# Loading K first, grouping the value products, and accumulating the output projection in PSUM in a one-core decode kernel

## The chip, the cores and the metric

The kernel runs on one core of one Trainium2 chip. Times are device microseconds (us) of a whole execution; a profile's "span" (from its first to its last instruction) is about 1.9 us shorter. The 16 runs of the kernel before lie between 85.12 and 85.53 us. Now and then a run takes longer, and only fast runs are compared. PE is TensorE, PEld its weight loads, DVE VectorE, ACT ScalarE, SP SyncE, which issues the transfers here.

## The reference

One decode step: layer norm of x (512 values), attention of 32 heads over a window of 1024 cached keys and values each, plus a feed-forward network, plus the residual.

```python
xn = _layernorm(x)                                  # x: 1 x 1 x 512
q = (xn @ wq)                                       # wq: 512 x 4096, 32 heads of 128
k, v = k_cache[:, :, Sk-W:, :], v_cache[:, :, Sk-W:, :]     # W = 1024 of Sk = 4096
o = softmax(q k^T * 128**-0.5) v                    # per head
A = o.reshape(1, 1, 4096) @ wo                      # wo: 4096 x 512
B = relu(xn @ w1 + b1)**2 @ w2 + b2                 # w1: 512 x 1376, w2: 1376 x 512
return x + A + B
```

Everything is bf16. Every weight and cache byte is used once: 28.0 MB are read, 8 MiB each for K and V, 4 MiB each for wq and wo, 2.7 MiB for w1 and w2.

## The kernel before

All large loads go out on one queue (SP) in the order wq, w1, w2, K, wo, V. PE transposes K (DVE copies each pair of heads back to SBUF), forms the scores, the softmax follows for all heads at once, and then the heads are taken one by one.

```python
small = ctx.enter_context(tc.tile_pool(name="small", bufs=1))     # many small tiles
wff   = ctx.enter_context(tc.tile_pool(name="wff", bufs=1))       # w1, w2
wbig  = ctx.enter_context(tc.tile_pool(name="wbig", bufs=4))      # wq, later wo
kv    = ctx.enter_context(tc.tile_pool(name="kv", bufs=1))        # K, V
# ... loads: wq, w1, w2, K (8 chunks of 4 heads), wo (4), V (16 chunks of 2 heads) ...
for h in range(Hq):
    g = h // 8
    for j in range(NJ):                                   # 8 matmuls, one column out
        nc.tensor.matmul(oT_ps[:, h : h + 1], lhsT=V_all[:, h, j, :], rhs=E[:, h, j : j + 1], ...)
    nc.vector.tensor_tensor(out=oTs[:, h : h + 1], in0=oT_ps[:, h : h + 1], in1=rb_sb[:, h : h + 1], op=ALU.mult)
    for bl in range(ND):                                  # 4 matmuls, each to its own column
        nc.tensor.matmul(attn_ps[:, bl, h : h + 1], lhsT=wo_t[g][:, h - 8 * g, bl * P : (bl + 1) * P],
                         rhs=oTs[:, h : h + 1], start=True, stop=True)
attn_sum = small.tile([P, ND], F32, name="attn_sum")
nc.vector.tensor_reduce(out=attn_sum[:, :], in_=attn_ps[:, :, :], axis=AX.X, op=ALU.add)
fin_bf = small.tile([P, ND], BF16, name="fin_bf")
nc.vector.tensor_tensor(out=fin_bf[:, :], in0=attn_sum[:, :], in1=ffn_ps[:, :], op=ALU.add)
# ... transpose on PE, copy to frow, transfer out ...
```

Note for later how the pools lie: the small tiles come first in each SBUF partition, each on a slot rounded up to 32 bytes (attn_sum has 16 bytes and takes 32), and the large tiles that the transfers fill lie directly behind them. The compiled program of the kernel before gives these start addresses in a partition: w1 at 22816, w2 at 33824, the four wq/wo buffers from 45088, K at 77856, V at 143392. Each is 32 more than a multiple of 256.

Of the kernel before, what the change touches and what calls it, by code (L numbers as in the profile page):

```python
# [9 lines left out]
ALU = mybir.AluOpType  # L10
AX = mybir.AxisListType
BF16 = mybir.dt.bfloat16
F32 = mybir.dt.float32
# [3 lines left out]
def kernel(  # L17
# [14 lines left out]
    nc = tc.nc  # L32
    P = 128

    _, _, D = A_x.shape
    _, Hkv, Sk, Dh = A_k_cache.shape
    Hq = 32
# [4 lines left out]
    Sk0 = Sk - W  # L42
    NJ = W // P
    ND = D // P
    NF = (F + P - 1) // P
    F_full = (NF - 1) * P
    F_last = F - F_full
    NG = Hq // 8
    KCH = 4
    VCH = 2  # L50
# [3 lines left out]
    dq = nc.sync  # L54
# [3 lines left out]
    small = ctx.enter_context(tc.tile_pool(name="small", bufs=1))  # L58
    wff = ctx.enter_context(tc.tile_pool(name="wff", bufs=1))
    wbig = ctx.enter_context(tc.tile_pool(name="wbig", bufs=4))  # L60
    kv = ctx.enter_context(tc.tile_pool(name="kv", bufs=1))
    ktsbp = ctx.enter_context(tc.tile_pool(name="ktsbp", bufs=2))
    psA = ctx.enter_context(tc.tile_pool(name="psA", bufs=1, space=bass.MemoryType.PSUM))

    wq_t = []
    for i in range(ND):
        t = wbig.tile([P, HD], BF16, name=f"wq{i}", tag="w")
        dq.dma_start(out=t[:, :], in_=A_wq[i * P : (i + 1) * P, :])
        wq_t.append(t)
    w1_sb = wff.tile([P, ND, F], BF16, name="w1_sb")  # L70
    dq.dma_start(out=w1_sb[:, :, :], in_=B_w1.rearrange("(i p) f -> p i f", p=P))
    w2_sb = wff.tile([P, NF, D], BF16, name="w2_sb")
    dq.dma_start(
        out=w2_sb[:, 0 : NF - 1, :],
        in_=B_w2[0:F_full, :].rearrange("(c p) d -> p c d", p=P),
    )
    dq.dma_start(out=w2_sb[0:F_last, NF - 1, :], in_=B_w2[F_full:F, :])  # L77
    K_all = kv.tile([P, Hq, NJ, Dh], BF16, name="K_all")
    for g in range(Hq // KCH):
        dq.dma_start(  # L80
            out=K_all[:, KCH * g : KCH * (g + 1), :, :],
            in_=A_k_cache[0, KCH * g : KCH * (g + 1), Sk0:Sk, :].rearrange("h (p j) d -> p h (j d)", p=P),
        )
    wo_t = []
    for g in range(NG):
        t = wbig.tile([P, 8, D], BF16, name=f"wo{g}", tag="w")
        dq.dma_start(out=t[:, :, :], in_=A_wo[g * 8 * Dh : (g + 1) * 8 * Dh, :].rearrange("(h d) c -> d h c", d=Dh))  # L87
        wo_t.append(t)
    V_all = kv.tile([P, Hq, NJ, Dh], BF16, name="V_all")
    for g in range(Hq // VCH):  # L90
        dq.dma_start(
            out=V_all[:, VCH * g : VCH * (g + 1), :, :],
            in_=A_v_cache[0, VCH * g : VCH * (g + 1), Sk0:Sk, :].rearrange("h (p j) d -> p h (j d)", p=P),
        )

    x_row = small.tile([1, D], BF16, name="x_row")
# [1 line left out]
    x4 = small.tile([ND, P], BF16, name="x4")  # L98
    dq2.dma_start(out=x4[:, :], in_=A_x[0, 0, :].rearrange("(c p) -> c p", p=P))  # L99
    b2_4 = small.tile([ND, P], BF16, name="b2_4")  # L100
# [6 lines left out]
    ident_bf = consts.tile([P, P], BF16, name="ident_bf")  # L107
# [11 lines left out]
    c_hT = c_b1T + NF  # L119
    c_qT = c_hT + NF  # L120
    assert c_qT + Hq <= 512
    aux_ps = psA.tile([P, 512], F32, name="aux_ps")
    S_ps = aux_ps[:, c_S : c_S + Hq * NJ].rearrange("p (h j) -> p h j", j=NJ)
    ffn_ps = psA.tile([P, ND], F32, name="ffn_ps")

    stats = small.tile([1, nc.vector.BN_STATS_DIM], F32, name="stats")
    nc.vector.bn_stats(out=stats[:, :], in_=x_row[:, :])
# [16 lines left out]
    b1T_sb = small.tile([P, NF], F32, name="b1T_sb")  # L144
    nc.vector.tensor_copy(out=b1T_sb[:, :], in_=aux_ps[:, c_b1T : c_b1T + NF])  # L145
    xnT = small.tile([P, ND], BF16, name="xnT")
    nc.vector.tensor_scalar(  # L147
        out=xnT[:, :],
        in0=aux_ps[:, c_xT : c_xT + ND],
        scalar1=mean_sb[:, 0:1],  # L150
        scalar2=rstd_sb[:, 0:1],
        op0=ALU.subtract,
        op1=ALU.mult,
    )

    for h in range(Hq):
        for i in range(ND):
            nc.tensor.matmul(  # L158
                aux_ps[:, c_qT + h : c_qT + h + 1],
                lhsT=wq_t[i][:, h * Dh : (h + 1) * Dh],  # L160
                rhs=xnT[:, i : i + 1],
                start=(i == 0),
                stop=(i == ND - 1),
            )
    qT_bf = small.tile([P, Hq], BF16, name="qT_bf")
    nc.vector.tensor_copy(out=qT_bf[:, :], in_=aux_ps[:, c_qT : c_qT + Hq])  # L166

    nc.vector.memset(aux_ps[:, c_hT : c_hT + NF], 0.0)  # L168
    for c in range(NF):
        ncol = P if c < NF - 1 else F_last  # L170
        for i in range(ND):
            nc.tensor.matmul(  # L172
                aux_ps[0:ncol, c_hT + c : c_hT + c + 1],
                lhsT=w1_sb[:, i, c * P : c * P + ncol],
                rhs=xnT[:, i : i + 1],
                start=(i == 0),
                stop=(i == ND - 1),
            )
    hb = small.tile([P, NF], F32, name="hb")
    nc.vector.tensor_tensor(out=hb[:, :], in0=aux_ps[:, c_hT : c_hT + NF], in1=b1T_sb[:, :], op=ALU.add)  # L180
    r2T = small.tile([P, NF], BF16, name="r2T")
    nc.vector.scalar_tensor_tensor(
        out=r2T[:, :], in0=hb[:, :], scalar=0.0, in1=hb[:, :], op0=ALU.max, op1=ALU.mult
    )
    for bl in range(ND):
        nc.tensor.matmul(ffn_ps[:, bl : bl + 1], lhsT=x4[:, :], rhs=ident_bf[0:ND, bl : bl + 1], start=True, stop=False)
        nc.tensor.matmul(ffn_ps[:, bl : bl + 1], lhsT=b2_4[:, :], rhs=ident_bf[0:ND, bl : bl + 1], start=False, stop=False)  # L187
        for c in range(NF):
            kc = P if c < NF - 1 else F_last
            nc.tensor.matmul(  # L190
                ffn_ps[:, bl : bl + 1],
                lhsT=w2_sb[0:kc, c, bl * P : (bl + 1) * P],
                rhs=r2T[0:kc, c : c + 1],
                start=False,
                stop=(c == NF - 1),
            )

    NPAIR = Hq // 2
    with tc.tile_pool(name="psK", bufs=2, space=bass.MemoryType.PSUM) as psK:
# [14 lines left out]
        for pp in range(NPAIR):  # L214
            kt_ps = psK.tile([P, 2, NJ, P], BF16, name="kt_ps", tag="kt")
            for hh in range(2):
                h = 2 * pp + hh
# [23 lines left out]
            out=Ssub[:, :, :],  # L241
            in0=S_ps,
            in1=mb_sb[:, :].unsqueeze(2).to_broadcast([P, Hq, NJ]),
            op=ALU.subtract,
        )
        E = small.tile([P, Hq, NJ], BF16, name="E")
# [11 lines left out]
        rb_sb = small.tile([P, Hq], F32, name="rb_sb")  # L258
        nc.vector.tensor_copy(out=rb_sb[:, :], in_=rb_ps[:, :])

    with tc.tile_pool(name="psV", bufs=1, space=bass.MemoryType.PSUM) as psV:
        oT_ps = psV.tile([P, Hq], F32, name="oT_ps")
        attn_ps = psV.tile([P, ND, Hq], F32, name="attn_ps")
        oTs = small.tile([P, Hq], BF16, name="oTs")
        for h in range(Hq):
            g = h // 8
            for j in range(NJ):
                nc.tensor.matmul(  # L268
                    oT_ps[:, h : h + 1],
                    lhsT=V_all[:, h, j, :],  # L270
                    rhs=E[:, h, j : j + 1],
                    start=(j == 0),
                    stop=(j == NJ - 1),
                )
            nc.vector.tensor_tensor(  # L275
                out=oTs[:, h : h + 1],
                in0=oT_ps[:, h : h + 1],
                in1=rb_sb[:, h : h + 1],
                op=ALU.mult,
            )  # L280
            for bl in range(ND):
                nc.tensor.matmul(  # L282
                    attn_ps[:, bl, h : h + 1],
                    lhsT=wo_t[g][:, h - 8 * g, bl * P : (bl + 1) * P],
                    rhs=oTs[:, h : h + 1],
                    start=True,
                    stop=True,
                )

        attn_sum = small.tile([P, ND], F32, name="attn_sum")  # L290
        nc.vector.tensor_reduce(out=attn_sum[:, :], in_=attn_ps[:, :, :], axis=AX.X, op=ALU.add)  # L291
        fin_bf = small.tile([P, ND], BF16, name="fin_bf")
        nc.vector.tensor_tensor(out=fin_bf[:, :], in0=attn_sum[:, :], in1=ffn_ps[:, :], op=ALU.add)
        frow_ps = psV.tile([ND, P], F32, name="frow_ps")
        nc.tensor.matmul(frow_ps[:, :], lhsT=fin_bf[:, :], rhs=ident_bf[:, :], start=True, stop=True)  # L295
        frow = small.tile([ND, P], BF16, name="frow")
        nc.vector.tensor_copy(out=frow[:, :], in_=frow_ps[:, :])  # L297
        dq.dma_start(out=out[0, 0, :].rearrange("(c p) -> c p", p=P), in_=frow[:, :])


# [28 lines left out]
```

## Time and profile before

| | before |
|---|---|
| time, median | 85.32 us |
| profile's span | 83.4 us |
| bytes read | 27.99 MB |
| first value matmul | 57.21 us |
| last V chunk landed (landing records of the trace) | 77.38 us |
| output transfer issued | 81.31 us |

Three rows of the page's 40 slices (2.09 us each), of the kernel before: PE's and the transfer engines' busy tenths, and the rate of the transfers.

```profile
PE   0000217970569999999999943143666666666640
DMA  3799999999999999999999999999999999995000
GB/s 48 299 422 429 432 396 412 383 355 339 382 385 391 381 384 388 388 380 386 386 355 348 353 343 348 354 380 387 380 382 387 386 382 386 385 388 182 0 8 0
```

The transfer engines are busy from the second slice to the 36th, PE is not: the stream of 28 MB sets the pace nearly to the end. The rate is about 430 GB/s while wq arrives in 8 KB pieces, about 385 for K and V in 2 KB pieces, and about 350 for wo in 1 KB pieces.

The windows view of the same kernel, for stretches in which only wq, K, wo and V arrive (columns: stretch and length, busy time and number of instructions of five engines, granted PE clock, share of the transfer engines, GB/s):

```profile
2.00:12.00 10.00, 1.09 (x9) 0.97 (x9) 1.62 (x6) 2.77 (x3) 0.00 (x0) 1.00 0.95 397
25.00:42.00 17.00, 17.00 (x350) 16.06 (x348) 13.38 (x11) 0.00 (x0) 0.00 (x0) 1.00 1.04 385
44.00:55.00 11.00, 6.30 (x131) 5.27 (x128) 7.20 (x12) 0.42 (x1) 0.00 (x0) 0.89 1.09 351
58.00:75.00 17.00, 10.95 (x291) 9.49 (x289) 3.88 (x24) 0.00 (x0) 0.00 (x0) 0.50 1.05 385
```

The timeline of the kernel before, one head of the value phase (start, duration, engine, line, what; in brackets the idle time ahead and what ended it), then the end:

```profile
74.99 0.29 PEld L268 LDWEIGHTS <-V_all 128*128 128x128 bf16 x8
75.01 0.35 PE L268 MATMUL oT_ps<-E,V_all 128*128 128x1 bf16 x8
75.40 0.16 DVE L275 TENSOR_TENSOR oTs<-oT_ps,rb_sb 128x1 bf16<-128x1 f32 x1 [0.55 <-PE oT_ps L268]
75.61 0.24 PE L282 MATMUL attn_ps<-oTs,wo 128*128 128x1 bf16 x4 [0.25 <-DVE oTs L275]
75.72 0.35 PE L268 MATMUL oT_ps<-E,V_all 128*128 128x1 bf16 x8
...
79.88 0.24 PE L282 MATMUL attn_ps<-oTs,wo 128*128 128x1 bf16 x4 [0.25 <-DVE oTs L275]
80.16 0.29 DVE L291 TENSOR_REDUCE attn_sum<-attn_ps 128x4 f32<-128x128 f32 x1 [0.33 <-PE attn_ps L282]
80.49 0.16 DVE L293 TENSOR_TENSOR fin_bf<-attn_sum,ffn_ps 128x4 bf16<-128x4 f32 x1
80.70 0.27 PE L295 MATMUL frow_ps<-ident_bf,fin_bf 128*4 128x128 bf16 x1 [0.58 <-DVE fin_bf L293]
81.00 0.28 DVE L297 CAST frow<-frow_ps 4x128 bf16<-4x128 f32 x1 [0.36 <-PE frow_ps L295]
81.31 0.33 SPq L298 DMA_DIRECT2D out_dram<-frow  x1
```

One head takes 0.71 us (75.01 to 75.72), of which PE idles 0.25 us for DVE. Two heads take 1.42 us while their chunk of V lands every 1.35 us, so PE falls slowly behind and finishes some 2.7 us after the last landing.

### The profile page before, as it was taken

How to read it: one execution, taken by the hardware profiler on the slowest of the kernel's cores; microseconds unless marked ns; L12 is line 12 of the kernel's file. 1: busy time of each engine (PE TensorE's matmuls, PEld its weight loads, DVE VectorE, ACT ScalarE, POOL GpSimd, SP SyncE). 2: the span in 40 equal slices, each digit the busy share in tenths (PEclk: the TensorE clock that was granted, in tenths of full speed). 3: DMA queues.
4: the chain of work that ended last, by engine and by line, in shares of the span. 5: the costliest groups of instructions: out<-in, count | busy, mean ns of one | idle time of the engine just before them, and what ended most of it. 6: DMA issues, size and time to landing. Idle time of an engine off the chain costs nothing.

```text
span 83.4 us, 2466 instructions
## 1 busy us (share of the span) xinstructions
PE 49.4 (59%) x1133; PEld 44.5 (53%) x1133; DVE 30.3 (36%) x70; ACT 3.4 (4%) x5; POOL 1.4 (2%) x11
## 2 busy tenths in 40 slices
PE   0000217970569999999999943143666666666640
PEld 0000207970459999999989931133555555555520
DVE  0300120010002789888978854421222222222240
ACT  0000580000000000000000000100000000000000
POOL 6000000000000000000000000000000000000000
PEclk9999999999999999999999999655555555555555
DMA  3799999999999999999999999999999999995000
GB/s 48 299 422 429 432 396 412 383 355 339 382 385 391 381 384 388 388 380 386 386 355 348 353 343 348 354 380 387 380 382 387 386 382 386 385 388 182 0 8 0
DMA packets 15306, 28.15 MB, mean 337 GB/s; under 512 B 607, under 2 KB 6080, under 8 KB 14784
## 3 DMA queue, kind: packets, MB, share of 16 engines
q1 hardware_dynamic: 15256, 27.99, 92.6%
q8 instruction: 9, 0.15, 0.7%
q10 hardware_dynamic: 40, 0.01, 0.0%
q14 instruction: 1, 0.01, 0.0%
HBM read 27.99 MB, written 0.00 MB: 336 GB/s over the span
## 4 chain that ended last, share of the span: by engine, by line
PE 43%; DMA 32%; SPq 10%; DVE 8%; issue 3%; ACTq 1%
PE kt_ps L219 18%; DMA K_all<-in_A_k_cache_dram 13%; DMA V_all<-in_A_v_cache_dram 13%; PE attn_ps L282 9%; PE oT_ps L268 9%; SPq L77 9%; PE aux_ps L205 7%; DVE oTs L275 7%; DMA b<-in_B_b_dram 6%; SPq L87 2%; ACTq L97 1%; DVE attn_sum L291 0%; PE frow_ps L295 0%; DVE frow L297 0%; ACTq L99 0%
## 5 line engine op out<-in xcount | busy, mean ns | idle before, releaser
L221 DVE COPY ktsb<-kt_ps 128x2048 bf16<-128x2048 bf16 x16 | 19.6, 1225 | 10.7 <-PE kt_ps L219 10.0
L219 PE MATMUL kt_ps<-ident_bf,K_all 128*128 128x128 bf16 x256 | 18.5, 230 | 0.9 <-DMA K_all<-in_A_k_cache_dram 0.8
L219 PEld LDWEIGHTS <-K_all 128*128 128x128 bf16 x256 | 16.0, 104 | 1.1 <-DMA K_all<-in_A_k_cache_dram 0.9
L282 PEld LDWEIGHTS <-wo 128*128 128x128 bf16 x128 | 8.4, 105 | 10.0 <-issue 10.0
L282 PE MATMUL attn_ps<-oTs,wo 128*128 128x1 bf16 x128 | 7.9, 165 | 8.1 <-DVE oTs L275 8.1
L268 PE MATMUL oT_ps<-E,V_all 128*128 128x1 bf16 x256 | 11.3, 165 | 1.6 <-DMA V_all<-in_A_v_cache_dram 1.6
L275 DVE TENSOR_TENSOR oTs<-oT_ps,rb_sb 128x1 bf16<-128x1 f32 x32 | 5.2, 162 | 18.8 <-PE oT_ps L268 18.8
L268 PEld LDWEIGHTS <-V_all 128*128 128x128 bf16 x256 | 9.3, 104 | 1.7 <-DMA V_all<-in_A_v_cache_dram 1.7
L205 PE MATMUL aux_ps<-qT_bf,ktsb 128*128 128x1 bf16 x256 | 9.0, 164 | 1.2 <-DVE ktsb L221 0.7
L205 PEld LDWEIGHTS <-ktsb 128*128 128x128 bf16 x256 | 7.7, 97 | 2.7 <-DVE ktsb L221 2.0
L158 PE MATMUL aux_ps<-xnT,wq 128*128 128x1 bf16 x128 | 3.7, 165 | 4.0 <-DVE xnT L147 2.4
L158 PEld LDWEIGHTS <-wq 128*128 128x128 bf16 x128 | 3.6, 104 | 4.0 <-issue 2.4
L190 PE MATMUL ffn_ps<-r2T,w_sb 128*128 128x1 bf16 (+1 forms) x44 | 2.0, 167 | 3.2 <-DMA w_sb<-in_B_w_dram 3.2
L142 PE MATMUL aux_ps<-ident_bf,x 4*128 4x4 bf16 x1 | 0.2, 183 | 5.7 <-DMA x<-in_A_x_dram 5.7
L190 PEld LDWEIGHTS <-w_sb 128*128 128x128 bf16 (+1 forms) x44 | 1.6, 105 | 3.4 <-DMA w_sb<-in_B_w_dram 3.2
L142 PEld LDWEIGHTS <-x 4*128 4x128 bf16 x1 | 0.1, 100 | 5.7 <-DMA x<-in_A_x_dram 5.7
L145 DVE COPY b1T_sb<-aux_ps 128x11 f32<-128x11 f32 x1 | 0.2, 170 | 5.5 <-PE ffn_ps L187 5.5
L166 DVE CAST qT_bf<-aux_ps 128x32 bf16<-128x32 f32 x1 | 0.2, 192 | 5.4 <-PE aux_ps L158 5.4
L247 ACT ACTIVATE E<-Ssub 128x256 bf16<-128x256 f32 x1 | 0.4, 416 | 41.0 <-DVE Ssub L240 41.0
L172 PE MATMUL aux_ps<-xnT,w_sb 128*128 128x1 bf16 (+1 forms) x44 | 1.5, 170 | 0.4 <-DVE aux_ps L168 0.4
L172 PEld LDWEIGHTS <-w_sb 128*128 128x128 bf16 (+1 forms) x44 | 1.5, 111 | 0.4 <-issue 0.3
L136 ACT ACT_TABLE_LOAD x1 | 1.3, 1283 | 9.2 <-DVE mean_sb L134 9.2
(52 smaller groups left out, 15.3 us busy)
## 6 DMA issues: line engine op xcount, KB each, us to landing
K_all<-in_A_k_cache_dram SPq DMA_DIRECT2D x8, 1024.0 KB, 14.3
V_all<-in_A_v_cache_dram SPq DMA_DIRECT2D x16, 512.0 KB, 10.8
wq<-in_A_wq_dram SPq DMA_DIRECT2D x4, 1024.0 KB, 7.1
wo<-in_A_wo_dram SPq DMA_DIRECT2D x4, 1024.0 KB, 12.3
w_sb<-in_B_w_dram SPq DMA_DIRECT2D x1, 1376.0 KB, 11.1
w_sb<-in_B_w_dram SPq DMA_DIRECT2D x1, 1280.0 KB
w_sb<-in_B_w_dram SPq DMA_DIRECT2D x1, 96.0 KB
x_row<-in_A_x_dram ACTq DMA_DIRECT2D x1, 1.0 KB
```

The source lines that it names most:

```text
L77: dq.dma_start(out=w2_sb[0:F_last, NF - 1, :], in_=B_w2[F_full:F, :])
L87: dq.dma_start(out=t[:, :, :], in_=A_wo[g * 8 * Dh : (g + 1) * 8 * Dh, :].rearrange("(h d) c -> d h c", d=Dh))
L136: nc.scalar.activation(out=std_sb[:, :], in_=statb_ps[:, 1:2], func=ACT.Sqrt, bias=eps_col[:, :], scale=1.0)
L158: nc.tensor.matmul(aux_ps[:, c_qT + h : c_qT + h + 1], lhsT=wq_t[i][:, h * Dh : (h + 1) * Dh], rhs=xnT[:, i : i + 1], start=(i == 0), stop ...
L172: nc.tensor.matmul(aux_ps[0:ncol, c_hT + c : c_hT + c + 1], lhsT=w1_sb[:, i, c * P : c * P + ncol], rhs=xnT[:, i : i + 1], start=(i == 0), ...
L190: nc.tensor.matmul(ffn_ps[:, bl : bl + 1], lhsT=w2_sb[0:kc, c, bl * P : (bl + 1) * P], rhs=r2T[0:kc, c : c + 1], start=False, stop=(c == N ...
L205: nc.tensor.matmul(S_ps[:, h, j : j + 1], lhsT=ktsb[:, hh, j, :], rhs=qT_bf[:, h : h + 1], start=True, stop=True,)
L219: nc.tensor.transpose(out=kt_ps[:, hh, j, :], in_=K_all[:, h, j, :], identity=ident_bf[:, :])
L221: nc.vector.tensor_copy(out=ktsb[:, :, :, :], in_=kt_ps[:, :, :, :])
L268: nc.tensor.matmul(oT_ps[:, h : h + 1], lhsT=V_all[:, h, j, :], rhs=E[:, h, j : j + 1], start=(j == 0), stop=(j == NJ - 1),)
L275: nc.vector.tensor_tensor(out=oTs[:, h : h + 1], in0=oT_ps[:, h : h + 1], in1=rb_sb[:, h : h + 1], op=ALU.mult,)
L282: nc.tensor.matmul(attn_ps[:, bl, h : h + 1], lhsT=wo_t[g][:, h - 8 * g, bl * P : (bl + 1) * P], rhs=oTs[:, h : h + 1], start=True, stop=True,
```

## The change

The intent: K first, so that the long K work starts sooner; the feed-forward network moved into the gap between softmax and V; the value phase in groups of four heads with the wo products one group late, so that PE does not wait for DVE in each head; the wo products and the network accumulated in the same PSUM columns, so that the final reduction and addition go; and the last V chunk in two halves.

```diff
+    K_all = kv.tile(...)                # K loads moved ahead of w1, w2
+    for g in range(Hq // KCH): dq.dma_start(out=K_all[...], ...)
     w1_sb = wff.tile([P, ND, F], BF16, name="w1_sb")
...
-    for g in range(Hq // VCH):
+    v_chunks = [(2 * g, 2 * g + 2) for g in range((Hq - 2) // VCH)] + [(Hq - 2, Hq - 1), (Hq - 1, Hq)]
+    for (ha, hb) in v_chunks:
...
-    (feed-forward matmuls after the q projection, into ffn_ps)
+    (the same matmuls after the softmax, w2's into fin_ps columns left open: stop=False)
...
-        attn_ps = psV.tile([P, ND, Hq], F32, name="attn_ps")
+        fin_ps = psV.tile([P, ND, 512], F32, name="fin_ps")
+        fincol = [fin_ps[:, bl, 0:1] for bl in range(ND)]
+        groups = [[gv * 4 + k for k in range(4)] for gv in range(7)] + [[28, 29], [30, 31]]
...
+        with tc.manual_schedule(engines={mybir.EngineType.PE}):
+            pv_group(groups[0])                     # value matmuls and one scaling per group
+            for gi in range(1, len(groups)):
+                pv_group(groups[gi])
+                wo_group(groups[gi - 1])            # wo matmuls, accumulating into fincol
+            wo_group(groups[-1])
-        attn_sum = small.tile([P, ND], F32, name="attn_sum")
-        nc.vector.tensor_reduce(out=attn_sum[:, :], in_=attn_ps[:, :, :], axis=AX.X, op=ALU.add)
         fin_bf = small.tile([P, ND], BF16, name="fin_bf")
-        nc.vector.tensor_tensor(out=fin_bf[:, :], in0=attn_sum[:, :], in1=ffn_ps[:, :], op=ALU.add)
+        nc.vector.tensor_copy(out=fin_bf[:, :], in_=fin_ps[:, :, 0])
```

More of the change, by code (lines that the diff above doesn't have):

```diff
@@ L69 @@
         wq_t.append(t)
+    K_all = kv.tile([P, Hq, NJ, Dh], BF16, name="K_all")
+    for g in range(Hq // KCH):
+        dq.dma_start(
+            out=K_all[:, KCH * g : KCH * (g + 1), :, :],
+            in_=A_k_cache[0, KCH * g : KCH * (g + 1), Sk0:Sk, :].rearrange("h (p j) d -> p h (j d)", p=P),
+        )
     w1_sb = wff.tile([P, ND, F], BF16, name="w1_sb")
@@ L77 @@
     dq.dma_start(out=w2_sb[0:F_last, NF - 1, :], in_=B_w2[F_full:F, :])
-    K_all = kv.tile([P, Hq, NJ, Dh], BF16, name="K_all")
-    for g in range(Hq // KCH):
-        dq.dma_start(
-            out=K_all[:, KCH * g : KCH * (g + 1), :, :],
-            in_=A_k_cache[0, KCH * g : KCH * (g + 1), Sk0:Sk, :].rearrange("h (p j) d -> p h (j d)", p=P),
-        )
     wo_t = []
@@ L89 @@
     V_all = kv.tile([P, Hq, NJ, Dh], BF16, name="V_all")
-    for g in range(Hq // VCH):
+    v_chunks = [(2 * g, 2 * g + 2) for g in range((Hq - 2) // VCH)] + [(Hq - 2, Hq - 1), (Hq - 1, Hq)]
+    for (ha, hb) in v_chunks:
         dq.dma_start(
-            out=V_all[:, VCH * g : VCH * (g + 1), :, :],
-            in_=A_v_cache[0, VCH * g : VCH * (g + 1), Sk0:Sk, :].rearrange("h (p j) d -> p h (j d)", p=P),
+            out=V_all[:, ha:hb, :, :],
+            in_=A_v_cache[0, ha:hb, Sk0:Sk, :].rearrange("h (p j) d -> p h (j d)", p=P),
         )
@@ L123 @@
     S_ps = aux_ps[:, c_S : c_S + Hq * NJ].rearrange("p (h j) -> p h j", j=NJ)
-    ffn_ps = psA.tile([P, ND], F32, name="ffn_ps")
     stats = small.tile([1, nc.vector.BN_STATS_DIM], F32, name="stats")
@@ L166 @@
     nc.vector.tensor_copy(out=qT_bf[:, :], in_=aux_ps[:, c_qT : c_qT + Hq])
-    nc.vector.memset(aux_ps[:, c_hT : c_hT + NF], 0.0)
-    for c in range(NF):
-        ncol = P if c < NF - 1 else F_last
-        for i in range(ND):
-            nc.tensor.matmul(
-                aux_ps[0:ncol, c_hT + c : c_hT + c + 1],
-                lhsT=w1_sb[:, i, c * P : c * P + ncol],
-                rhs=xnT[:, i : i + 1],
-                start=(i == 0),
-                stop=(i == ND - 1),
-            )
-    hb = small.tile([P, NF], F32, name="hb")
-    nc.vector.tensor_tensor(out=hb[:, :], in0=aux_ps[:, c_hT : c_hT + NF], in1=b1T_sb[:, :], op=ALU.add)
-    r2T = small.tile([P, NF], BF16, name="r2T")
-    nc.vector.scalar_tensor_tensor(
-        out=r2T[:, :], in0=hb[:, :], scalar=0.0, in1=hb[:, :], op0=ALU.max, op1=ALU.mult
-    )
-    for bl in range(ND):
-        nc.tensor.matmul(ffn_ps[:, bl : bl + 1], lhsT=x4[:, :], rhs=ident_bf[0:ND, bl : bl + 1], start=True, stop=False)
-        nc.tensor.matmul(ffn_ps[:, bl : bl + 1], lhsT=b2_4[:, :], rhs=ident_bf[0:ND, bl : bl + 1], start=False, stop=False)
-        for c in range(NF):
-            kc = P if c < NF - 1 else F_last
-            nc.tensor.matmul(
-                ffn_ps[:, bl : bl + 1],
-                lhsT=w2_sb[0:kc, c, bl * P : (bl + 1) * P],
-                rhs=r2T[0:kc, c : c + 1],
-                start=False,
-                stop=(c == NF - 1),
-            )
     NPAIR = Hq // 2
@@ L259 @@
         nc.vector.tensor_copy(out=rb_sb[:, :], in_=rb_ps[:, :])
+    nc.vector.memset(aux_ps[:, c_hT : c_hT + NF], 0.0)
+    for c in range(NF):
+        ncol = P if c < NF - 1 else F_last
+        for i in range(ND):
+            nc.tensor.matmul(
+                aux_ps[0:ncol, c_hT + c : c_hT + c + 1],
+                lhsT=w1_sb[:, i, c * P : c * P + ncol],
+                rhs=xnT[:, i : i + 1],
+                start=(i == 0),
+                stop=(i == ND - 1),
+            )
+    hb = small.tile([P, NF], F32, name="hb")
@@ L261 @@
+    nc.vector.tensor_tensor(out=hb[:, :], in0=aux_ps[:, c_hT : c_hT + NF], in1=b1T_sb[:, :], op=ALU.add)
+    r2T = small.tile([P, NF], BF16, name="r2T")
+    nc.vector.scalar_tensor_tensor(
+        out=r2T[:, :], in0=hb[:, :], scalar=0.0, in1=hb[:, :], op0=ALU.max, op1=ALU.mult
+    )
     with tc.tile_pool(name="psV", bufs=1, space=bass.MemoryType.PSUM) as psV:
         oT_ps = psV.tile([P, Hq], F32, name="oT_ps")
-        attn_ps = psV.tile([P, ND, Hq], F32, name="attn_ps")
-        oTs = small.tile([P, Hq], BF16, name="oTs")
@@ L265 @@
-        for h in range(Hq):
-            g = h // 8
-            for j in range(NJ):
-                nc.tensor.matmul(
-                    oT_ps[:, h : h + 1],
-                    lhsT=V_all[:, h, j, :],
-                    rhs=E[:, h, j : j + 1],
-                    start=(j == 0),
-                    stop=(j == NJ - 1),
-                )
+        fin_ps = psV.tile([P, ND, 512], F32, name="fin_ps")
+        fincol = [fin_ps[:, bl, 0:1] for bl in range(ND)]
+        for bl in range(ND):
+            nc.tensor.matmul(fincol[bl], lhsT=x4[:, :], rhs=ident_bf[0:ND, bl : bl + 1], start=True, stop=False)
+            nc.tensor.matmul(fincol[bl], lhsT=b2_4[:, :], rhs=ident_bf[0:ND, bl : bl + 1], start=False, stop=False)
+            for c in range(NF):
+                kc = P if c < NF - 1 else F_last
+                nc.tensor.matmul(
+                    fincol[bl],
+                    lhsT=w2_sb[0:kc, c, bl * P : (bl + 1) * P],
+                    rhs=r2T[0:kc, c : c + 1],
+                    start=False,
+                    stop=False,
+                )
@@ new lines, with pv_group @@
+        oTs = small.tile([P, Hq], BF16, name="oTs")
+        groups = [[gv * 4 + k for k in range(4)] for gv in range(7)] + [[28, 29], [30, 31]]
+        def pv_group(heads):
+            for h in heads:
+                for j in range(NJ):
+                    nc.tensor.matmul(
+                        oT_ps[:, h : h + 1],
+                        lhsT=V_all[:, h, j, :],
+                        rhs=E[:, h, j : j + 1],
+                        start=(j == 0),
+                        stop=(j == NJ - 1),
+                    )
+            h0, h1 = heads[0], heads[-1] + 1
@@ L275 @@
             nc.vector.tensor_tensor(
-                out=oTs[:, h : h + 1],
-                in0=oT_ps[:, h : h + 1],
-                in1=rb_sb[:, h : h + 1],
+                out=oTs[:, h0:h1],
+                in0=oT_ps[:, h0:h1],
+                in1=rb_sb[:, h0:h1],
                 op=ALU.mult,
             )
-            for bl in range(ND):
-                nc.tensor.matmul(
-                    attn_ps[:, bl, h : h + 1],
-                    lhsT=wo_t[g][:, h - 8 * g, bl * P : (bl + 1) * P],
-                    rhs=oTs[:, h : h + 1],
-                    start=True,
-                    stop=True,
-                )
@@ L290, with wo_group @@
-        attn_sum = small.tile([P, ND], F32, name="attn_sum")
-        nc.vector.tensor_reduce(out=attn_sum[:, :], in_=attn_ps[:, :, :], axis=AX.X, op=ALU.add)
+        def wo_group(heads):
+            for h in heads:
+                g = h // 8
+                for bl in range(ND):
+                    nc.tensor.matmul(
+                        fincol[bl],
+                        lhsT=wo_t[g][:, h - 8 * g, bl * P : (bl + 1) * P],
+                        rhs=oTs[:, h : h + 1],
+                        start=False,
+                        stop=(h == Hq - 1),
+                    )
@@ L292 @@
+        with tc.manual_schedule(engines={mybir.EngineType.PE}):
[4 more added lines that the diff above has]
+            wo_group(groups[-1])
         fin_bf = small.tile([P, ND], BF16, name="fin_bf")
-        nc.vector.tensor_tensor(out=fin_bf[:, :], in0=attn_sum[:, :], in1=ffn_ps[:, :], op=ALU.add)
-        frow_ps = psV.tile([ND, P], F32, name="frow_ps")
-        nc.tensor.matmul(frow_ps[:, :], lhsT=fin_bf[:, :], rhs=ident_bf[:, :], start=True, stop=True)
+        nc.vector.tensor_copy(out=fin_bf[:, :], in_=fin_ps[:, :, 0])
@@ L296 @@
+        frow_ps = aux_ps[0:ND, 0:P]
+        nc.tensor.matmul(frow_ps, lhsT=fin_bf[:, :], rhs=ident_bf[:, :], start=True, stop=True)
         frow = small.tile([ND, P], BF16, name="frow")
-        nc.vector.tensor_copy(out=frow[:, :], in_=frow_ps[:, :])
+        nc.vector.tensor_copy(out=frow[:, :], in_=frow_ps)
         dq.dma_start(out=out[0, 0, :].rearrange("(c p) -> c p", p=P), in_=frow[:, :])
```

## The prediction

> **What bounds the kernel now.** The transfers do, almost to the end. The slices row of the page shows the 16 transfer engines at 9 tenths or more from about 4 us to 75 us; 28.0 MB arrive at some 385 GB/s (348 GB/s while the 1 KB pieces of wo arrive). The landing records show the last V chunk complete at 77.4 us of the 83.4 us span. [...] the 16 parts of the last chunk land between 75.7 and 77.4 us.
>
> What follows the stream is the exposed part. From 57.2 us the timeline repeats one head every 0.711 us: eight value matmuls, a wait for the 0.16 us DVE scaling (0.25 us of PE idle in each head, 8.1 us in the list of groups), four wo matmuls. Two heads take 1.42 us, a chunk lands every 1.35 us, so PE falls behind: head 30 starts at 78.56 us, 1.2 us after its chunk landed. Then come two heads, a 0.29 us reduction, add, transpose, copy, and the output transfer (issued at 81.31, end 83.4).
>
> **What the change does.**
> 1. K before w1/w2: K processing should start near 16.7 us instead of 24.8 and end near 42.5 instead of 50.4. But V must still come after the same 19.5 MB, so its first chunk still lands near 57 us. The 8 us become PE waiting for V. Worth about 0.
> 2. The FFN moves between softmax and V; its 88 matmuls (about 3 us) and weights (landed by about 43 us) fit before 57 us. Worth 0.
> 3. Groups of four heads, with wo one group late: PE's cost per two heads falls to about 0.7 us [...] plus part of one DVE wait, well under 1.35 us. PE waits for each chunk; the 1.2 us lag goes.
> 4. wo accumulates in PSUM with the FFN: the reduction (0.29 us + 0.04) goes; a 128x4 copy replaces the add.
> 5. The last chunk is halved: head 30's matmuls run before head 31 lands.
>
> Bytes and packet sizes are unchanged, so I leave the stream's end at 77.4 us.
>
> **The new tail**, from durations read in the old trace: last landing 77.4; eight matmuls until DVE starts 0.41; DVE to PE 0.22; eight wo matmuls until DVE 0.40 (four took 0.28); copy 0.21; transpose 0.30; copy to issue 0.31; output transfer to end 2.1. Sum 81.4 us against 83.4: 2.0 us less. All of it is on the critical path; the rest of the 8 us of DVE waits is worth nothing, since PE would wait for the stream instead.
>
> **Predicted:** 83.3 us (85.3 - 2.0), range 82.5 to 84.2. Faster by over 2% (under about 83.6): 0.64; within 2%: 0.34; slower by over 2%: 0.02.
>
> **What would show it.** First V matmul still near 57 us; K's first transpose near 16.7; the 32 waits of wo matmuls on DVE gone; value matmuls waiting for V transfers in most chunks; chain of waits ending in V transfer, one short group, copy, transpose, output; last landing within 0.5 us of 77.4.
>
> **What would make it wrong.** The stream's end moving: the 1.7 us spread between engines appears first with w2 (0.3 us for w1, 1.6 us for w2), and w2 now runs elsewhere; without the spread the end would come up to 0.8 us earlier, with a gap in the queue later. Or value groups waiting for DVE (each group's first matmul is ordered behind the previous group's scaling) adding to the tail. A few tenths decide the class.

Two passages are cut. One was a general statement about when a transfer counts as complete; what the trace shows is that the 16 parts of the first V chunk land between 55.41 and 57.16 us, and the first value matmul starts at 57.21. The other gave a spacing of matmuls that the trace does not show: in the value phase of the old trace their starts lie 27 ns apart (median), so that 24 take 0.65 us, near the 0.7 that stands there as the author's estimate. The tail's sum: 77.4 + 0.41 + 0.22 + 0.40 + 0.21 + 0.30 + 0.31 + 2.1 come to 81.4 us.

## The result, and the profile after

The changed kernel takes 79.22 us (median of 8 runs, 79.14 to 79.36) against 85.32 us: 6.1 us less, where 2.0 had been predicted. The ratio is 0.9287, with a 95% interval of 0.9275 to 0.9298. Ratios here are the mean time of one kernel's fast runs over the mean of the other's fast runs of the same rounds, so not quite the ratio of the medians.

| | before | predicted | after |
|---|---|---|---|
| first K transpose | 24.76 us | 16.7 | 16.33 us |
| first value matmul | 57.21 us | near 57 | 54.04 us |
| last V chunk landed | 77.38 us | 77.4 | 73.34 us |
| from there to the span's end | 6.0 us | 4.0 | 4.1 us |
| span | 83.4 us | 81.4 | 77.4 us |

The tail is as predicted. The other 4.0 us are in the row that the prediction left unchanged: the end of the stream.

The same three rows of the page, of the changed kernel (slices of 1.93 us):

```profile
PE   0001212999999999999975387300537664766850
DMA  2799999999999999999999999999999999999300
GB/s 34 279 441 408 428 432 392 409 406 411 395 407 413 401 408 408 398 414 409 377 384 384 382 384 383 389 401 389 410 407 407 410 408 397 408 409 384 138 8 1
```

The windows view of the changed kernel, for stretches in which wq, K, wo and V arrive:

```profile
2.00:12.00 10.00, 1.07 (x7) 0.93 (x7) 1.62 (x6) 3.03 (x4) 0.00 (x0) 1.00 0.97 402
17.00:34.00 17.00, 16.86 (x351) 15.82 (x349) 13.47 (x11) 0.00 (x0) 0.00 (x0) 1.00 1.05 406
43.00:52.00 9.00, 3.99 (x94) 3.75 (x94) 2.24 (x11) 0.42 (x1) 0.00 (x0) 0.55 1.09 387
54.50:71.50 17.00, 10.03 (x304) 8.96 (x302) 1.09 (x7) 0.00 (x0) 0.00 (x0) 0.50 1.05 405
```

wq arrives as before (397 and 402 GB/s, over a stretch that includes the slow start). K and V come at 405 instead of 385, wo at 387 instead of 351, with the same bytes in the same pieces and the engines equally busy (the share column stays at 1.05 and 1.09). The trace's record of each piece says the same: from 13 us on, the mean for a 2 KB piece of K or V fell from 88.6 to 84.4 ns, for a 1 KB piece of wo or w2 from 50.9 to 46.2 ns. Before, their tenth percentile was 84 and 46 ns too, but the slowest tenth took 94 and 56 or more; after, nearly all take exactly 84 and 46. A V chunk lands every 1.28 us instead of 1.35.

The end of the chain of waits, in order of time, and the timeline behind it, of the changed kernel:

```profile
54.01 10.24 DMA V_all<-in_A_v_cache_dram
64.27 9.07 DMA V_all<-in_A_v_cache_dram
73.39 0.37 PE oT_ps L270 x8
73.76 0.21 PE fin_ps L289 x8
74.01 0.36 PE fin_ps L289 x8
```

```profile
73.80 0.16 DVE L278 TENSOR_TENSOR oTs<-oT_ps,rb_sb 128x2 bf16<-128x2 f32 x1 [0.97 <-PE oT_ps L270]
74.40 0.16 DVE L305 CAST fin_bf<-fin_ps 128x4 bf16<-128x4 f32 x1 [0.44 <-PE fin_ps L289]
74.61 0.27 PE L307 MATMUL aux_ps<-ident_bf,fin_bf 128*4 128x128 bf16 x1 [0.26 <-DVE fin_bf L305]
74.92 0.28 DVE L309 CAST frow<-aux_ps 4x128 bf16<-4x128 f32 x1 [0.36 <-PE aux_ps L307]
75.23 0.33 SPq L310 DMA_DIRECT2D out_dram<-frow  x1
```

PE now waits for V in nearly every chunk (15 times for 17 transfers, by the list of waits), eight value matmuls follow the last landing at 73.34 us, and the chain to the output is the one that was added up in advance: 0.41 us to the scaling (73.39 to 73.80), 0.21 to wo (74.01), 0.39 to the copy (74.40), 0.83 to the output's issue (75.23).

### The profile page after: what moved, and what is told of

It reads as the page before. It is cut to its first block, busy times and chain, and to the rows that moved or that the text cites. A ratio compares the mean times of both kernels' runs of the same rounds, so it can differ in the third digit from the quotient of the medians.

```text
span 77.4 us, 2442 instructions
## 1 busy us (share of the span) xinstructions
PE 46.5 (60%) x1133; PEld 42.6 (55%) x1133; DVE 26.1 (34%) x46; ACT 3.4 (4%) x5; POOL 1.4 (2%) x11
## 4 chain that ended last, share of the span: by engine, by line
DMA 51%; PE 38%; DVE 3%; SPq 2%; issue 2%; DVEq 0%
DMA V_all<-in_A_v_cache_dram 37%; PE kt_ps L189 21%; DMA wq<-in_A_wq_dram 14%; PE aux_ps L175 9%; PE aux_ps L158 5%; SPq L68 2%; DVE ktsb L191 2%; PE fin_ps L289 1%; SPq L87 1%; DVE m L198 1%; PE m1T_ps L200 1%; PE mb_ps L206 1%; PE oT_ps L270 0%; DVE m_col L202 0%; PE aux_ps L307 0%
## 5 line engine op out<-in xcount | busy, mean ns | idle before, releaser
L270 PE MATMUL oT_ps<-E,V_all 128*128 128x1 bf16 x256 | 9.5, 166 | 12.4 <-DMA V_all<-in_A_v_cache_dram 12.3
L270 PEld LDWEIGHTS <-V_all 128*128 128x128 bf16 x256 | 8.1, 105 | 13.7 <-DMA V_all<-in_A_v_cache_dram 13.7
L278 DVE TENSOR_TENSOR oTs<-oT_ps,rb_sb 128x4 bf16<-128x4 f32 (+1 forms) x9 | 1.5, 162 | 24.5 <-PE oT_ps L270 24.5
L289 PE MATMUL fin_ps<-oTs,wo 128*128 128x1 bf16 x128 | 4.7, 165 | 0.0
L289 PEld LDWEIGHTS <-wo 128*128 128x128 bf16 x128 | 4.1, 104 | 0.1
L235 PEld LDWEIGHTS <-w_sb 128*128 128x128 bf16 (+1 forms) x44 | 1.5, 111 | 0.9 <-issue 0.9
L127 DVE BATCH_NORM_STATS2 stats<-x_row 1x6 f32<-1x512 bf16 x1 | 0.7, 681 | 2.0 <-DMA x_row<-in_A_x_dram 2.0
L257 PE MATMUL fin_ps<-r2T,w_sb 128*128 128x1 bf16 (+1 forms) x44 | 1.3, 165 | 0.0
```

The lines of the kernel that those rows point to most:

```text
L235: nc.tensor.matmul(aux_ps[0:ncol, c_hT + c : c_hT + c + 1], lhsT=w1_sb[:, i, c * P : c * P + ncol], rhs=xnT[:, i : i + 1], start=(i == 0), ...
L257: nc.tensor.matmul(fincol[bl], lhsT=w2_sb[0:kc, c, bl * P : (bl + 1) * P], rhs=r2T[0:kc, c : c + 1], start=False, stop=False,)
L278: nc.vector.tensor_tensor(out=oTs[:, h0:h1], in0=oT_ps[:, h0:h1], in1=rb_sb[:, h0:h1], op=ALU.mult,)
L289: nc.tensor.matmul(fincol[bl], lhsT=wo_t[g][:, h - 8 * g, bl * P : (bl + 1) * P], rhs=oTs[:, h : h + 1], start=False, stop=(h == Hq - 1),)
```

## The experiments

Why does the stream run faster? The diff has no line about it, but it removes a tile: attn_sum, 16 bytes in each partition on a slot of 32. Everything behind it moves down by 32 bytes. The compiled program of the changed kernel has w1 at 22784, K at 77824 and V at 143360: each now a multiple of 256.

The address theory: transfers into SBUF are slower where the destination starts off a coarse address grid. That, and 256 bytes as the grid, was the author's guess, which no run had shown yet. It fits the addresses: all the large tiles of the changed kernel start at a multiple of 256 (w1, at 22784, at no multiple of 512), all those of the slow kernel 32 bytes past one. Whether the grid is as coarse as that is what e5 and e6 ask.

The rivals: the new order of the loads, or quieter engines in the value phase, or some state of chip or program.

All kernels computed the right result. There were three rounds for e1 to e8 and five for the others.

**e1: the old kernel, only moved onto the grid.** frow is the last small tile ahead of w1; widening it adds no instruction.

```diff
-        frow = small.tile([ND, P], BF16, name="frow")
+        frow = small.tile([ND, P + 112], BF16, name="frow")      # 224 bytes; frow[:, 0:P] is used
```

> The kernel before with the last small tile (frow) widened by 224 bytes, so that w1, w2, wq/wo, K and V start at a multiple of 256 bytes in their partition and not 32 bytes past one; no instruction is added. Address theory: V chunks land 1.28 us apart and not 1.35, first V matmul near 54 us and not 57.2; PE, at 0.711 us a head, is then further behind the stream, so about 26.2 us from there to the end stay: span near 80.1 us, time near 82.0. Rival, the order of the loads (K first) makes the transfers fast: no change, 85.3 us, V chunks still 1.35 us apart. Rival, the shorter value phase (PE and DVE disturbing the transfers less): no change either.

Measured: ratio 0.9645 (0.9609 to 0.9682), that is 82.3 us of 85.33; one of the four runs was slow (83.31 us) and is left out. The windows view of this run, K and then V (the stretches are those of the kernel before and of the changed kernel; the last 1.5 us of the K stretch already bring wo), and the first value matmul:

```profile
25.00:42.00 17.00, 17.00 (x371) 15.86 (x369) 14.40 (x12) 0.00 (x0) 0.00 (x0) 1.00 1.05 402
54.50:71.50 17.00, 11.04 (x288) 9.59 (x288) 3.82 (x24) 0.00 (x0) 0.00 (x0) 0.50 1.05 405
```

```profile
54.05 0.37 PE L268 MATMUL oT_ps<-E,V_all 128*128 128x1 bf16 x8 [0.42 <-DMA V_all<-in_A_v_cache_dram]
54.78 0.35 PE L268 MATMUL oT_ps<-E,V_all 128*128 128x1 bf16 x8
```

The stream is as fast as in the changed kernel, its last landing at 73.34 us to the hundredth, with the old order of loads and the old value phase. The time fell by 3.0 us and not by the 4.0 that the stream gained: heads still take 0.71 us each, so after the first V chunk (3.16 us earlier) PE sets the pace, and its last wo product ends about 3.6 us after the last landing.

**e2: the changed kernel, moved off the grid again** (the same edit with 32 bytes).

> The changed kernel with frow widened by 32 bytes, so that all the large tiles start 32 bytes past a multiple of 256, as they did before the change. Address theory: V chunks 1.35 us apart again, last landing near 77.4 us, time near 83.3 (the number that was predicted). Rivals (order of loads, or calmer engines): stays at 79.2.

Measured: 83.49 us, ratio 0.9793 (0.9767 to 0.9818; whether it is more than 2% faster than the kernel before is unclear). Its windows, K and then V:

```profile
17.00:34.00 17.00, 16.99 (x340) 16.22 (x339) 12.84 (x11) 0.00 (x0) 0.00 (x0) 1.00 1.04 385
58.00:75.00 17.00, 9.42 (x281) 8.44 (x282) 0.97 (x6) 0.00 (x0) 0.00 (x0) 0.50 1.05 387
```

The slow stream is back and ends at 77.36 us, against 77.38 before. This is the kernel that the prediction described without knowing it: 83.3 had been said. Neither the order of loads nor the quieter value phase makes the transfers fast.

**e3: control, moved by 256 bytes** (the same edit with 256).

> Control: the changed kernel with frow widened by 256 bytes: every large tile moves, but by a multiple of 256. Address theory: 79.2 us as the changed kernel. If any shift or the wider tile costs something: slower than 79.2.

Measured: 79.35 us, ratio 0.9293 (0.9263 to 0.9324), as the changed kernel. A shift as such costs nothing. Its profile fell in a slow state (81.34 us) and is not compared. It shows one thing, though: in it K came at 406 GB/s (17 to 34 us) and V at 373 (54.5 to 71.5 us), with every large tile on the grid. In this execution the slow state thus slowed the later part of the stream and not the earlier.

**e4: V alone off the grid.**

```diff
-    V_all = kv.tile([P, Hq, NJ, Dh], BF16, name="V_all")
+    V_buf = kv.tile([P, Hq * NJ * Dh + 16], BF16, name="V_buf")
+    V_all = V_buf[:, 16:].rearrange("p (h j d) -> p h j d", j=NJ, d=Dh)
```

> Dose: the changed kernel with V alone (and the K transposes' SBUF tile behind it, which no transfer writes) 32 bytes past a multiple of 256; w, wo and K stay aligned. Address theory: K chunks still 2.57 us apart, V chunks 1.35 and not 1.28, so last landing and time some 16 x 0.07 = 1.1 us later: near 80.4 us. [...]

Measured: 80.29 us, ratio 0.9411 (0.9387 to 0.9436). Its windows, K, wo and V:

```profile
17.00:34.00 17.00, 17.00 (x356) 15.99 (x354) 13.47 (x11) 0.00 (x0) 0.00 (x0) 1.00 1.05 406
43.00:52.00 9.00, 3.99 (x94) 3.75 (x94) 2.12 (x10) 0.42 (x1) 0.00 (x0) 0.56 1.09 388
54.50:71.50 17.00, 9.43 (x282) 8.36 (x279) 0.97 (x6) 0.00 (x0) 0.00 (x0) 0.50 1.05 387
```

Within one execution K and wo come fast (406 and 388) and V slowly (387). The last landing is 74.36 us, 1.0 later than in the changed kernel. One profile alone would not exclude a slow state, as e3's shows; but all four runs lie between 80.12 and 80.49 us, at the 80.4 that was forecast.

**e5 and e6: how coarse is the grid?** The changed kernel moved by 64 and by 128 bytes.

> How coarse is the grid? The changed kernel with frow widened by 64 bytes: large tiles start 64 bytes past a multiple of 256. If only odd multiples of 32 are slow (a 64-byte grid): V chunks 1.28 us apart and 79.2 us. If every start off the 256-byte grid is slow[...]: V chunks 1.35 us apart and 83.4 us.

> The same with 128 bytes. 64-byte grid or 128-byte grid: 79.2 us. 256-byte grid: 83.4 us. If e5 is slow and this is fast, the grid is 128 bytes.

Measured: 83.17 us, ratio 0.9742 (0.9724 to 0.9761), and 82.93 us, ratio 0.9718 (0.9696 to 0.9741). Both have V at 386 GB/s, with last landings at 77.25 and 77.03 us; the windows of e5 and then of e6:

```profile
58.00:75.00 17.00, 9.48 (x283) 8.50 (x284) 0.97 (x6) 0.00 (x0) 0.00 (x0) 0.50 1.05 386
58.00:75.00 17.00, 9.64 (x290) 8.67 (x291) 0.97 (x6) 0.00 (x0) 0.00 (x0) 0.50 1.05 386
```

Offsets of 32, 64 and 128 all cost nearly the full 4 us (by the medians 4.3, 4.0 and 3.7); offset 0 does not, whether K and V start at an even multiple of 256 (the changed kernel) or at an odd one (e1 and e3). As far as these offsets show, the grid for the start of a tile is 256 bytes; other offsets were not run.

**e7: the order of loads undone** (w1 and w2 ahead of K again, addresses kept).

> The changed kernel with the order of loads undone (w1 and w2 before K again), all tiles still on the 256-byte grid. Prediction's step 1 and the address theory: 79.2 us; K's work starts some 8 us later and ends near 49 us, softmax and FFN near 55 us, against a first V chunk at 54 us, so PE starts V about 1 us late and catches up at about 0.6 us a chunk: no change of the end. Rival, the order gave part of the 6 us: over 80 us.

Measured: 79.28 us, ratio 0.9283 (0.9262 to 0.9305), with one run of four slow (80.57 us): no change. Its first value matmuls on the timeline:

```profile
56.60 0.99 PE L270 MATMUL oT_ps<-E,V_all 128*128 128x1 bf16 x32
57.85 0.99 PE L270 MATMUL oT_ps<-E,V_all 128*128 128x1 bf16 x32 [0.25 <-DVE oTs L278]
```

PE starts V 2.6 us later than in the changed kernel (54.04), takes two chunks (32 matmuls) at once, and has caught up by 60.7 us, where it waits for V again; the last landing is 73.33 us. I had expected about 1 us of delay, so that detail was off, and the conclusion stands: K first bought slack, not time.

**e8: the value phase head by head**, with everything else of the change kept.

```diff
-        groups = [[gv * 4 + k for k in range(4)] for gv in range(7)] + [[28, 29], [30, 31]]
+        groups = [[h] for h in range(Hq)]
-            (value matmuls of a group, then wo matmuls of the group before)
+            for grp in groups:
+                pv_group(grp)
+                wo_group(grp)
```

> The changed kernel with the value phase head by head as before (eight value matmuls, scaling, four wo matmuls, PE waiting for DVE in each head); accumulation in PSUM, order of loads and aligned tiles stay. PE takes 0.711 us a head, 1.42 per chunk, against 1.28 us per chunk of the faster stream: from 53.9 us 32 heads end near 76.7 and not 74.4: about 81.5 us. That is what the grouping is worth with the fast stream; if it is worth only the 1.7 us that the prediction counted for it with the slow stream: 80.9. If PE follows the stream anyway: 79.6.

Measured: 82.01 us, ratio 0.9619 (0.9588 to 0.9650). From its timeline:

```profile
76.80 0.35 PE L270 MATMUL oT_ps<-E,V_all 128*128 128x1 bf16 x8
77.19 0.16 DVE L278 TENSOR_TENSOR oTs<-oT_ps,rb_sb 128x1 bf16<-128x1 f32 x1 [0.55 <-PE oT_ps L270]
77.40 0.24 PE L289 MATMUL fin_ps<-oTs,wo 128*128 128x1 bf16 x4 [0.25 <-DVE oTs L278]
```

The grouping is worth about 2.8 us with the fast stream (82.0 against the 79.2 of the changed kernel), 0.5 more than I expected. I had left out that the last head's wo products take until 0.3 us after their start; the rest is not taken apart. The profiled run was also the slowest of its four, and its stream ran late although V lies on the grid: V came at 377 GB/s, the first V matmul at 54.72 us and not 54.04, the last landing at 75.13. The worth of the grouping is therefore taken from the median of the four runs, not from this profile.

**e9: the last chunk whole again.**

```diff
-    v_chunks = [(2 * g, 2 * g + 2) for g in range((Hq - 2) // VCH)] + [(Hq - 2, Hq - 1), (Hq - 1, Hq)]
+    v_chunks = [(2 * g, 2 * g + 2) for g in range(Hq // VCH)]
```

> The changed kernel with the last V chunk whole again (512 KB for heads 30 and 31). Prediction's step 5: head 30's eight matmuls then run after the last landing: 0.23 us more, near 79.45. If the split is worth nothing (the landing of the whole chunk is no later): 79.2.

Measured: 79.48 us, ratio 0.9312 (0.9292 to 0.9331). That is about 0.2 us over the changed kernel (0.9287 and 0.9288), as counted, but the intervals overlap slightly. The profiles show the part that step 5 names: from the first value matmul behind the last landing to the scaling it takes 0.63 us (73.50 to 74.13), in the changed kernel 0.41.

**e10: a version meant to beat both.** wo is loaded after V, so that behind the last landing stand four wo matmuls alone, without value matmuls and scaling.

```diff
-    (wo loads, then V loads)
+    (V loads, then wo loads; the last wo tile in pieces of 4, 2, 1 and 1 heads)
-            (pv_group of one group, then wo_group of the one before)
+            for grp in groups:
+                pv_group(grp)
+            for grp in groups:
+                wo_group(grp)
```

> A version meant to beat both: wo is loaded after V, its last tile in four pieces (the last one head), and PE does all value groups before the wo groups. The stream stays (28 MB, aligned), last landing near 73.4 us; behind it come four wo matmuls (0.28 us) and no value matmuls, scaling or eight wo matmuls (1.0 us from the first to the copy in the changed kernel): 0.7 us less, 78.5 us. If the landing comes later for the small pieces of wo at the end: 79.0 or more.

Measured: 78.80 us, ratio 0.9241 (0.9207 to 0.9276), with one run slow.

**e11 and e12: the two again, on one chip.**

> The changed kernel, unaltered, beside the version with wo last on one chip, since those two stood in different calls: 79.2 us.

> The version with wo last once more: 78.7 us, 0.5 us under the changed kernel beside it. If its first result was luck of the chip: 79.2.

Measured: 79.28 us, ratio 0.9288 (0.9266 to 0.9309), and 78.63 us, ratio 0.9223 (0.9199 to 0.9248). From e12's timeline:

```profile
72.44 1.64 PE L294 MATMUL fin_ps<-oTs,wo 128*128 128x1 bf16 x32 [0.34 <-DMA wo<-in_A_wo_dram]
74.11 0.16 DVE L309 CAST fin_bf<-fin_ps 128x4 bf16<-128x4 f32 x1 [10.61 <-PE fin_ps L294]
74.94 0.32 SPq L314 DMA_DIRECT2D out_dram<-frow  x1
```

The last piece of wo lands at 73.77 us, 0.4 later than V's last did in the changed kernel, and the copy starts 0.34 us after it instead of 1.06. But this profile is of one of the slower runs (78.92 us). In e10's, of its fastest run (78.57 us), the last piece lands at 73.43 us, only 0.1 later, and the copy starts 0.35 us after it. So some 0.6 us of the 0.7 remain, as the medians say (79.28 - 78.63 = 0.65): the best of all versions, 0.7% under the changed kernel and 7.8% under the kernel before.

## Why the prediction was wrong

The four corners, as ratios to the kernel before, with its median of 85.33 us:

| | large tiles 32 bytes off | large tiles on the grid |
|---|---|---|
| old value phase and order | 1 (85.3 us) | 0.9645 (82.3 us, e1) |
| new value phase and order | 0.9793 (83.6 us, e2) | 0.9293 (79.3 us, e3) |

- **What bounds the kernel: right.** The stream does; the four corners confirm it.
- **Step 1, K first, worth 0: right.** e7.
- **Step 2, the network in the gap, worth 0: in agreement.** On the changed kernel's timeline its last matmuls end at 49.0 us and the first V chunk lands at 54.0. It was not taken apart by itself.
- **Step 3, grouping takes PE's lag away: right, and more than counted.** It was sized for the slow stream. With the fast one, PE head by head would be slower than the stream by 0.14 us a chunk (1.42 against 1.28) and not by 0.07. e8 gives 2.8 us. This is also why the restructuring and the new addresses are worth more together (6.0 us) than one by one (3.0 and 1.8).
- **Steps 4 and 5, the shorter tail: right in sum.** Predicted 4.0 us from the last landing, measured 4.1 in the changed kernel. For step 5 see e9; step 4 was not run by itself, but the reduction ahead of the copy (80.16 to 80.49 in the old timeline) is gone. Taken together the restructuring was predicted at 2.0 us; e2 shows about 1.8 without the address effect.
- **The step that failed** is the sentence "Bytes and packet sizes are unchanged, so I leave the stream's end at 77.4 us." The stream ended at 73.34 us. Removing a 16-byte tile moved every large destination from 32 bytes past a 256-byte boundary onto it. e1 and e2 show that this alone moves the stream's end by 4.0 us in either kernel, e4 that it acts per destination, e3, e5 and e6 that of the shifts by 64, 128 and 256 bytes only that by 256 keeps the fast stream. Without it the changed kernel takes 83.2 to 83.7 us (e2), within the range given.
- **The doubt that was named was the wrong one.** I feared the 1.7 us spread between the engines' landings, and put it down to w2. In the changed kernel the spread appears with the third K chunk, long before w2 arrives, and is again 1.7 us at the end (in both traces the 16 landings of a large transfer lie within 0.6 us up to some 18 us, and 1.6 to 1.9 us apart from 20 us on). So w2 is not its cause. The traces hold a candidate: queue q8 brings instructions in nine packets of 16 KB ("q8 instruction: 9, 0.15" on the page), about 1 us each (0.88 to 1.28 us in the changed kernel). In all profiles the first starts between 18.3 and 19.2 us, and the next large landing is the first in which one of the 16 parts comes about 1.4 us late; after each of the next four packets one more part is late. In e7 the second packet starts at 32.5 us (25.4 in the changed kernel), and the second late part appears at 36.7 us (29.7). That fits, but no run took the packets away.

Two things could have told in advance: the start addresses of the large tiles in the two compiled programs, and the old profile's rates, which fell with the size of the pieces (430, 385, 350 GB/s for 8, 2 and 1 KB), by more than they do on the grid (430, 405, 387).

What stays open: the mechanism. Off the grid a 2 KB piece took 88.6 against 84.4 ns, 5% more, and a 1 KB piece 50.9 against 46.2 ns, 10% more: some 4 to 5 ns a piece in both cases. The 8 KB pieces of wq, also off the grid before, showed a median of 309 ns in both kernels. That many pieces off the grid still took the fast time, and others 10 ns longer, is seen but not explained.

The pieces of w1 speak against the start of each single piece as the cause. Its four pieces of 2752 bytes lie end to end in a partition, so with w1 on the grid they start 0, 192, 128 and 64 bytes past a multiple of 256; moved by 64 or 128 bytes (e5, e6) they start at the same four offsets in another order. On the grid nearly all 512 pieces took 109 ns (changed kernel and e1); in e5 and e6 the mean was 112.1 ns and under half took 109, also while nothing but w1 was arriving (in the kernel before, 32 bytes off: 111.6 ns, and 262 of 512 took 109). That the start of the whole run in a partition counts would fit, and was not tested; nor was whether it is the destination's address alone or its offset against the source's, since no source was moved.

## What to carry to other kernels

Where transfers set the pace, as they did here, look up the start address of every large SBUF destination in the compiled program, and put large tiles on a 256-byte grid by their own means (large pools first, or a padded small pool), since a small tile added or removed ahead of them can shift them all. Here a 16-byte tile shifted them by 32 bytes, and starts 32, 64 or 128 bytes off the grid cost 3.7 to 4.3 us of 79; no other kernel was measured. When a change moves the time by more than its parts explain, compare rates and single pieces of the same transfers in both traces before looking for a cause in the lines of the diff. What an engine's speed-up is worth depends on the pace of what it follows: the grouping was worth 2.8 us with the fast stream (e8), while with the slow one the whole restructuring gave 1.8 us (e2).
